# Attention, ELU layer and maxout layer on one core: the engines' orders in the attention stage written out step by step

## The chip, the cores and the metric

The kernel runs on one core of one Trainium2 chip. The metric is the device time of one execution in microseconds (us); lower is better. Three timed runs of the kernel before gave 537.43, 546.26 and 544.27 us, median 544.27 us.

## The reference

```python
# attention: batch 2, 12 heads, 448 tokens, head size 64, fp32
scores = q @ k.T / sqrt(64), causal mask, softmax along the row
x = (attn @ v), heads side by side              # 896 x 768
# first layer: w_in 768 x 2048, w_out 2048 x 768, given in float64
h = x @ w_in
g = where(h > 0, h, exp(min(h, 0)) - 1)         # ELU
x = g @ w_out
# second layer: w1, w2, w3, w_out 768 x 768, given in float64
h = maximum(maximum(x @ w1, x @ w2), x @ w3)
out = h @ w_out                                 # 896 x 768, fp32
```

## The kernel before, in words

**Attention.** The 24 heads are worked in 12 pairs (numbered 0 to 11; 0 to 5 are batch 0). A head has 448 rows, in 4 chunks of 112. A pair goes through these steps, each a small function:

- `load_qk`, `load_v`: transfers of q, k, v on SyncE's queue (SP), the first k on ScalarE's.
- `qk_pe(p, w)`: four TensorE (PE) transposes of q (w=0) or k (w=1) into PSUM (tiles `tq`, `tk`). `qk_copy(p, w)` takes them to SBUF (tile `qk`, three buffers).
- `s_pe(p, g)`: score matmuls of chunk group g, (3), (2, 0) or (1), for both heads (tiles `s`). Four PSUM banks, so two groups at a time.
- `s_max(p, j, c)` on VectorE (DVE, L229): mask, row minimum of the negated scores, result to SBUF tile `e`. `s_exp` on ScalarE (ACT, L243): the exponential with the row's sum. `r_inv` (DVE, L255 and L256): the reciprocals. `e_norm` on GpSimd (POOL, L262): division by the sum.
- `t_pe(p, j, g)`: PE transposes of `e` (tiles `te`, 10 blocks of 112 x 112 a head in groups of 2, 4 and 4). `t_copy` takes them to SBUF (tile `et`).
- `av_pe(p)`: 16 matmul records with v (tile `av`, a single PSUM bank). `x_hi` (ACT, L310) and `x_lo` (DVE, L315) split it into two parts for the next layer (tile `xT`).

The transposes `tq`, `tk` and `te` share three PSUM banks.

**Early part of the first layer.** `d_load`, `d_conv1`, `d_conv2`, `d_hi`, `d_lo` fetch blocks 0 and 1 of w_in and turn float64 into two fp32r parts (tiles `raw_l`, `c_l`, `ws_l`); `d_pe(f, part)` are 12 parts of three matmuls for batch 0 (tile `ph`); `d_elu` and `d_split` are the ELU and the split of its result (tiles `e`, `g`, `gs`).

**What sets the order.** Attention and the early part run under `manual_schedule`: an engine executes its instructions in the order in which the program issues them. In `ORDER` (L414) each kind of step has a number; pair p's step stands at p plus that number, and an engine's line is the sorted list, so that all pairs have the same pattern. `JOIN` (L477) gives the early steps absolute places. `NEEDS` holds a step back in the program until the steps before it are issued. After attention the rest of the first layer, the product with w_out (`py`) and the second layer (`pm`, `po`) are ordered by the tile scheduler. Its first unit is block 0 with batch 1; it uses, as its PSUM bank, the one that `av` had.

Of the kernel before, what the change touches and what calls it, by code (L numbers as in the profile page):

```python
# [9 lines left out]
F32R = mybir.dt.float32r  # L10
# [19 lines left out]
def tile_attention_elu_maxout(  # L30
# [13 lines left out]
    nc = tc.nc  # L44
# [138 lines left out]
    def qk_copy(p, w):  # L183
        if p not in qk_t:
            qk_t[p] = hd.tile([P, 2, S], F32, tag="qk", bufs=3, name=f"qk{p}")
        t = ps_now.pop(("qk", p, w))
        if w == 0:
            nc.scalar.activation(qk_t[p][:, w, :], t[:, :S], AF.Copy, scale=SCALE)  # L188
        else:
            nc.vector.tensor_copy(qk_t[p][:, w, :], t[:, :S])  # L190

    PASSES = ((0, 1),)

# [84 lines left out]
        ps_now["t", h, g] = t[:C, :n], slice(TOFF[grp[0]], TOFF[grp[0]] + n)  # L278


    T_ACT = ((0, 1), (0, 1))
# [38 lines left out]
    def load_win(f, key):  # L320
        raw_t[key] = load64(key, w_in[:, f * P : (f + 1) * P], NW)
# [13 lines left out]
                )  # L335
            yield

    def elu_first(f, b, ph):
# [29 lines left out]

    def d_load(f):
        load_win(f, f"l{f}")  # L370

    def d_conv1(f):
        early["c", f] = conv_first(f"l{f}", raw_t.pop(f"l{f}"), NW)

    def d_conv2(f):
        (low, r), _, high = early.pop(("c", f))
        early["w", f] = conv_last(low, r, high)

    def d_hi(f):
        ws_t[f] = weight_tile(f"l{f}")  # L380
# [12 lines left out]
        if part == KD - 1:  # L393
            drain(early.pop(("gen", f)))

    def d_elu(f):
        early["g", f] = elu_first(f, 0, early.pop(("ps", f)))

    def d_split(f):
        elu_last(f, 0, early.pop(("g", f)), g_early)  # L400

    def drain(gen):
        for _ in gen:
# [2 lines left out]
    def spin(n):  # L406
        for _ in range(n):
# [3 lines left out]

    ORDER = {  # L414
        "SP": {
            (load_qk,): -3.413,
            (load_v,): 0.204,
        },
        "PE": {
            (s_pe, 0): 0.209,  # L420
            (t_pe, 0, 0): 2.025,
            (t_pe, 0, 1): 2.050,
            (s_pe, 1): 0.241,
            (t_pe, 0, 2): 2.323,
            (t_pe, 1, 0): 2.260,
            (s_pe, 2): 0.396,
# [36 lines left out]
            (x_hi,): 3.973,
        },
        "POOL": {
            (e_norm, 0, 3): 1.068,
            (e_norm, 0, 2): 0.924,
            (e_norm, 0, 1): 0.712,
            (e_norm, 0, 0): 1.029,
            (e_norm, 1, 3): 0.153,  # L470
            (e_norm, 1, 2): 0.687,
            (e_norm, 1, 1): 0.924,
            (e_norm, 1, 0): 0.871,
        },
    }

    JOIN = {  # L477
        "SP": {
            (d_load, 0): -0.691,
            (d_load, 1): 3.094,  # L480
            (d_load, 2): 8.233,
        },
        "ACT": {
            (d_conv1, 0): 2.804,
            (d_hi, 0): 3.210,
            (d_conv1, 1): 6.478,
            (d_hi, 1): 9.132,
            (d_elu, 0): 14.736,
            (d_split, 0): 15.039,
            (d_elu, 1): 15.473,  # L490
            (d_split, 1): 15.548,
        },
        "DVE": {
            (d_conv2, 0): 3.345,
            (d_lo, 0): 5.619,
            (d_conv2, 1): 7.954,
            (d_lo, 1): 9.620,
        },
        "PE": {
            (d_pe, 0, 0): 12.269,  # L500
            (d_pe, 0, 1): 12.755,
            (d_pe, 0, 2): 13.105,
            (d_pe, 0, 3): 13.174,
            (d_pe, 0, 4): 13.501,
            (d_pe, 0, 5): 13.589,
            (d_pe, 1, 0): 12.444,
            (d_pe, 1, 1): 14.334,
            (d_pe, 1, 2): 14.066,
            (d_pe, 1, 3): 14.757,
            (d_pe, 1, 4): 14.356,  # L510
            (d_pe, 1, 5): 15.145,
        },
    }


    G_OF = {c: g for g, grp in enumerate(GROUPS_S) for c in grp}
    BOTH = [(j, c) for j in range(2) for c in range(NCH)]
    NEEDS = {
        load_qk: lambda p: [(s_pe, p - 4, 2)],
        load_v: lambda p: [(av_pe, p - 5)],  # L520
        qk_pe: lambda p, w: [(load_qk, p)],
        qk_copy: lambda p, w: [(qk_pe, p, w), (s_pe, p - 3, 2)],
        s_pe: lambda p, g: [(qk_copy, p, 0), (qk_copy, p, 1)]
        + [(s_max, p - (g < 2), j, c) for j in range(2) for c in GROUPS_S[(g + 1) % 3]],
        s_max: lambda p, j, c: [(s_pe, p, G_OF[c]), (t_pe, p - 3, j, 2)],
        s_exp: lambda p, j, c: [(s_max, p, j, c)],
        r_inv: lambda p, j: [(s_exp, p, j, c) for c in range(NCH)],
        e_norm: lambda p, j, c: [(r_inv, p, j)],
        t_pe: lambda p, j, g: [(e_norm, p, j, c) for c in range(min(GROUPS_T[g]), NCH)],
        t_copy: lambda p, j, g: [(t_pe, p, j, g), (av_pe, p - 2)],  # L530
        av_pe: lambda p: [(t_copy, p, j, g) for j in range(2) for g in range(3)]
        + [(x_lo, p - 1)],
        x_hi: lambda p: [(av_pe, p)],
        x_lo: lambda p: [(x_hi, p)],
        d_load: lambda f: [],
        d_conv1: lambda f: [(d_load, f)],
        d_conv2: lambda f: [(d_conv1, f)],
        d_hi: lambda f: [(d_conv2, f)],
        d_lo: lambda f: [(d_hi, f)],
        d_pe: lambda f, part: [(d_lo, f)]  # L540
        + [(s_max, NH // 2 - 1, j, c) for j, c in BOTH],
        d_elu: lambda f: [(d_pe, f, KD - 1)],
        d_split: lambda f: [(d_elu, f)],
    }


    FREES = {
        qk_pe: lambda p, w: (qk_copy, p, w),
        t_pe: lambda p, j, g: (t_copy, p, j, g),
    }  # L550

    def queues():
        for e, steps in ORDER.items():
            line = [(p + at, f, (p, *w)) for (f, *w), at in steps.items() for p in range(NH // 2)]
            line += [(at, f, tuple(w)) for (f, *w), at in JOIN.get(e, {}).items()]
            yield [x[1:] for x in sorted(line, key=lambda x: x[0])]


    with tc.manual_schedule():

        still = const.tile([P, 512], BF16, name="still")
        nc.vector.memset(still, 0.0)
        idle = bank("x", "idle")
        spin(8)

        waiting, issued, frees = list(queues()), set(), [None] * BANKS["t"]
        while any(waiting):
            before = len(issued)
            for line in waiting:
                while line:  # L570
                    f, args = line[0]
                    needs = NEEDS[f](*args) + [frees[turn["t"]]] * (f in FREES)
                    if not all(x in issued for x in needs if x and x[1] >= 0):
                        break
                    if f in FREES:
                        frees[turn["t"]] = FREES[f](*args)
# [179 lines left out]
```

## Time and profile before

| what | value |
|---|---|
| three runs | 537.43, 546.26, 544.27 us; median 544.27 us |
| span of the profiled execution | 537.8 us |
| its own time | the page gives none beside the span; the lowest run is 537.43 us, so what lies around the span is taken as nothing |
| PE busy | 517.2 us (96%) |
| DVE, ACT, POOL busy | 320.2 (60%), 251.7 (47%), 48.5 (9%) us |
| begin of the uninterrupted layer work on PE | 130.27 us |

The last 407.5 us are nearly uninterrupted layer matmuls; the work that the change touches lies in the first 130 us. Shares of busy time over the whole span therefore say little about it. The views by stretch and the chain of waits do.

### The profile page before, as it was taken

How to read it: one execution, taken by the hardware profiler on the slowest of the kernel's cores; microseconds unless marked ns; L12 is line 12 of the kernel's file. 1: busy time of each engine (PE TensorE's matmuls, PEld its weight loads, DVE VectorE, ACT ScalarE, POOL GpSimd, SP SyncE). 2: the span in 40 equal slices, each digit the busy share in tenths (PEclk: the TensorE clock that was granted, in tenths of full speed). 3: DMA queues.
4: the chain of work that ended last, by engine and by line, in shares of the span. 5: the costliest groups of instructions: out<-in, count | busy, mean ns of one | idle time of the engine just before them, and what ended most of it. 6: DMA issues, size and time to landing. Idle time of an engine off the chain costs nothing.

```text
span 537.8 us, 7380 instructions
## 1 busy us (share of the span) xinstructions
PE 517.2 (96%) x2785; PEld 449.1 (84%) x2785; DVE 320.2 (60%) x657; ACT 251.7 (47%) x539; POOL 48.5 (9%) x104
## 2 busy tenths in 40 slices
PE   7869989996999999999999999999999999999997
PEld 3545655675999999999999999999999999999997
DVE  3656888735797778765555555635998857711000
ACT  4657869844576556653332332323544424301111
POOL 1522544520000000000000000000000000000000
PEclk9787999998999999999999999999999999999999
DMA  9932462000456322223333334412566353000111
GB/s 206 218 71 60 96 171 78 18 1 6 121 168 177 99 82 81 84 69 117 100 110 104 118 117 123 152 60 63 205 212 225 118 175 119 1 1 15 62 71 60
DMA packets 75461, 55.53 MB, mean 103 GB/s; under 512 B 34465, under 2 KB 74657, under 8 KB 75425
## 3 DMA queue, kind: packets, MB, share of 16 engines
q1 hardware_dynamic: 74496, 54.83, 34.5%
q8 instruction: 22, 0.36, 0.3%
q10 hardware_dynamic: 928, 0.23, 0.2%
q14 instruction: 15, 0.11, 0.1%
HBM read 52.30 MB, written 2.75 MB: 102 GB/s over the span
## 4 chain that ended last, share of the span: by engine, by line
PE 86%; ACT 9%; DVE 3%; DMA 1%; issue 1%; DVEq 0%; ACTq 0%; SPq 0%
PE pm L333 24%; PE py L636 22%; PE ph L333 22%; PE po L333 8%; ACT e L243 6%; PE s L209 4%; PE te L272 3%; PE av L299 2%; DVE e L229 1%; PE idle L408 1%; DMA raw_l<-in_moe_w_in_dram 1%; ACT et L289 1%; ACT qk L188 1%; DVE c_l L108 0%; PE tk L174 0%
## 5 line engine op out<-in xcount | busy, mean ns | idle before, releaser
L333 PE MATMUL pm<-yT,ws_m 128*128 128x448 f32 x648 | 131.5, 365 | 0.0
L333 PEld LDWEIGHTS pm<-yT,ws_m 128*128 128x128 f32 x648 | 121.7, 188 | 9.6
L333 PE MATMUL ph<-xT,ws_l 128*128 128x448 f32 x576 | 121.4, 372 | 3.8 <-DVE xT L315 3.8
L333 PEld LDWEIGHTS ph<-xT,ws_l 128*128 128x128 f32 x576 | 109.8, 192 | 13.6 <-DVE xT L315 4.2
L636 PE MATMUL py<-gs,ws_o 128*128 128x448 f32 x576 | 116.9, 365 | 0.0
L636 PEld LDWEIGHTS py<-gs,ws_o 128*128 128x128 f32 x576 | 108.2, 188 | 8.5
L243 ACT ACTIVATE e<-e,nm 112x224 f32<-112x224 f32 (+2 forms) x96 | 49.5, 518 | 20.0 <-DVE nm L229 20.0
L262 POOL TENSOR_SCALAR e<-e,r 112x448 f32<-112x448 f32 (+3 forms) x96 | 47.2, 517 | 65.0 <-DVE r L256 40.5
L229 DVE CUSTOM_DVE_ANT_0 e<-s,mask 112x336 f32<-112x336 f32 (+2 forms) x96 | 37.5, 443 | 12.4 <-PE s L209 12.4
L333 PE MATMUL po<-w2s,h 128*128 128x384 f32 x252 | 43.9, 334 | 0.0
L333 PEld LDWEIGHTS po<-w2s,h 128*128 128x128 f32 x252 | 43.7, 188 | 0.0
L272 PE MATMUL te<-ident,e 112*112 112x112 f32 x240 | 33.0, 272 | 5.8 <-ACT qk L188 2.9
L209 PE MATMUL s<-qk 64*112 64x448 f32 (+3 forms) x192 | 34.8, 478 | 3.5 <-ACT qk L188 2.6
L272 PEld LDWEIGHTS te<-ident,e 112*112 112x112 f32 x240 | 24.1, 137 | 14.1 <-issue 6.6
L128 ACT ACTIVATE ws_o<-c_o 128x512 fp32r<-128x512 f32 x24 | 15.1, 629 | 40.5 <-PE py L636 40.5
L209 PEld LDWEIGHTS s<-qk 64*112 64x112 f32 x192 | 18.0, 197 | 17.5 <-issue 8.3
L107 DVE SCALAR_TENSOR_TENSOR c_m<-c_m,raw_m 128x768 uint32<-128x768 uint32 x24 | 22.9, 955 | 15.5 <-ACT c_m L102 15.3
L102 ACT ACTIVATE c_m<-raw_m 128x768 f32<-128x768 f32 x24 | 21.8, 907 | 20.9 <-DVE ws_m L129 15.3
L129 DVE TENSOR_TENSOR ws_o<-c_o,ws_o 128x512 fp32r<-128x512 f32 x24 | 16.5, 689 | 19.3 <-ACT ws_o L128 19.2
L128 ACT ACTIVATE gs<-g 128x448 fp32r<-128x448 f32 x32 | 18.3, 571 | 20.1 <-DVE g L344 20.1
L128 ACT ACTIVATE ws_m<-c_m 128x768 fp32r<-128x768 f32 x18 | 15.2, 845 | 26.2 <-PE pm L333 12.8
L129 DVE TENSOR_TENSOR gs<-g,gs 128x448 fp32r<-128x448 f32 x32 | 19.9, 622 | 11.8 <-ACT gs L128 11.7
(55 smaller groups left out, 488.6 us busy)
## 6 DMA issues: line engine op xcount, KB each, us to landing
raw_m<-in_moe_w_dram SPq DMA_DIRECT2D x18, 768.0 KB, 4.3
raw_l<-in_moe_w_in_dram SPq DMA_DIRECT2D x16, 768.0 KB, 4.7
raw_o<-in_moe_w_out_dram SPq DMA_DIRECT2D x24, 512.0 KB, 3.5
raw_m<-in_moe_w_out_dram SPq DMA_DIRECT2D x6, 768.0 KB, 4.2
qn<-in_q_dram SPq DMA_DIRECT2D x24, 112.0 KB, 3.3
vn<-in_v_dram SPq DMA_DIRECT2D x12, 224.0 KB, 3.3
out_dram<-o SPq DMA_DIRECT2D x14, 192.0 KB, 1.9
kn<-in_k_dram SPq DMA_DIRECT2D x22, 112.0 KB, 3.2
```

The lines of the kernel that those rows point to most:

```text
L102: nc.scalar.activation(f32(r), f32(high), AF.Copy, scale=BIAS),
L107: nc.vector.scalar_tensor_tensor(r, r, 3, low, ALU.logical_shift_left, ALU.bitwise_or)
L128: nc.scalar.activation(hi, src, AF.Copy)
L129: nc.vector.tensor_tensor(lo, src, f32(hi), ALU.subtract)
L209: nc.tensor.matmul(s[j][:C, o : o + (c + 1) * C], qk[:, a, c * C : (c + 1) * C], qk[:, c2, : (c + 1) * C], start=(w == 0 and n == 0), stop ...
L229: nc.vector.tensor_tensor_reduce(out=e_t[h][:, EOFF[c] : EOFF[c] + (c + 1) * C], in0=ps_now.pop(("s", h, c)), in1=mask[:, (NCH - 1 - c) * ...
L243: nc.scalar.activation(e, e, AF.Exp, bias=nm_t[h][:, c : c + 1], scale=-1.0, accum_out=sm_t[p][:, j, c : c + 1],)
L262: nc.gpsimd.tensor_scalar(e, e, ps_now["r", h][:, c : c + 1], 1.0, ALU.mult, ALU.mult)
L272: nc.tensor.transpose(t[:C, n : n + C], e[:, EOFF[c] + j * C : EOFF[c] + (j + 1) * C], ident[:C, :C],)
L299: nc.tensor.matmul(a[j * D : (j + 1) * D, kc * C : S], vn[:, j * NCH + kc, :], et[j][:, TOFF[kc] : TOFF[kc] + S - kc * C], start=(n == 0), ...
L333: nc.tensor.matmul(ps, w(a, kc), x(c, kc), start=(i == 0), stop=(i == len(seq) - 1))
L636: nc.tensor.matmul(py[b][:, :S], w[:, a, kc * P : (kc + 1) * P], g_sp[hk * HK + kc, b][:, c, :], start=(hk == 0 and i == 0), stop=(hk == N ...
```

## The change: what it does

The numbers of `ORDER` and `JOIN` are replaced by `PLAN`, a list for each engine in which each step of each pair stands by itself (a letter for the step, then pair, head or part, and group, in hexadecimal). The pattern can differ from pair to pair. Which engine makes a copy follows from the list in which it stands: 13 of 24 `qk_copy` are on ACT (12 before) and 42 of 72 `t_copy` (48 before). `d_conv1` and `d_conv2` are cut into `d_scale`, `d_shift`, `d_join`; `d_elu` and `d_split` into `d_exp`, `d_max`, `d_ghi`, `d_glo`. The early load of block 2 is left to the scheduler. `NEEDS` and the new `holds` only restate which buffers and banks are in use. What is computed, and the number of matmuls, transposes and copies, stays. On PE the number of places where a step of another kind follows (transposes, scores, `av`, early matmuls) is 66; it was 77. Of these, 25 (before 36) lead into transposes.

```diff
-        if w == 0:
-            nc.scalar.activation(qk_t[p][:, w, :], t[:, :S], AF.Copy, scale=SCALE)
+        o, t = qk_t[p][:, w, :], t[:, :S]
+        if on_act(qk_copy, p, w):
+            nc.scalar.activation(o, t, AF.Copy, scale=SCALE if w == 0 else 1.0)
+        elif w == 0:
+            nc.vector.tensor_scalar(o, t, SCALE, None, ALU.mult)
         else:
-            nc.vector.tensor_copy(qk_t[p][:, w, :], t[:, :S])
+            nc.vector.tensor_copy(o, t)
...
-        if g in T_ACT[j]:
+        if on_act(t_copy, p, j, g):
...
-    ORDER = {
-        "SP": {
-            (load_qk,): -3.413,
-            (load_v,): 0.204,
...
+    PLAN = {
+        "SP": """
+            L0 L1 L2 L3 V0 V1 R0 L4 R1 L5 V2 L6 V3 L7 V4 L8 V5 L9 V6 LA V7 LB V8 V9 VA VB
+            """,
+        "PE": """
+            Q00 Q01 Q11 S02 S00 S01 Q10 Q21 Q20 S12 S11 Q31 Q30 S10 S20 T001 T000 T002 S21 S22
...
+    def on_act(f, *args):
+        return (f, args) in plan["ACT"]
...
+        waiting = [list(line) for line in plan.values()]
```

Three places show what moves. The first is PE after the first pair's scores (`tq1`, `tk1` are q and k of pair 1; `s2`, `s3` the scores of pair 1's heads; `te0` the first transposes of head 0). Before:

```order
L209 MATMUL s0_2_174<-qk0_147 112x224
L209 MATMUL s1_2_175<-qk0_147 112x224
L174 MATMUL tq1_178<-ident_58,qn1_110 128x112 x4
L174 MATMUL tk1_183<-ident_58,kn1_113 128x112 x4
L209 MATMUL s2_0_220<-qk1_195 112x448
L209 MATMUL s3_0_221<-qk1_195 112x448
```

Now:

```order
L174 MATMUL tq1_193<-ident_58,qn1_110 128x112 x4
L174 MATMUL tk2_198<-ident_58,kn2_119 128x112 x4
L174 MATMUL tq2_203<-ident_58,qn2_116 128x112 x4
L212 MATMUL s2_2_236<-qk1_157 112x224
L212 MATMUL s3_2_237<-qk1_157 112x224
L212 MATMUL s2_1_240<-qk1_157 112x336
```

The transposes of pair 2's q and k now stand ahead of pair 1's scores, and pair 3's ahead of the last group of pair 1; k of pair 1 stands ahead of pair 0's scores.

The second is ACT around a copy of q in the middle of attention (`qk6` belongs to pair 6, `e12` and `e13` are its heads; in the second list `qk8` is two pairs later than `e12`). Before:

```order
L243 ACTIVATE e10_646,sm5_648<-e10_646,nm10_647 112x224
L243 ACTIVATE e11_650,sm5_648<-e11_650,nm11_651 112x336
L243 ACTIVATE e11_650,sm5_648<-e11_650,nm11_651 112x224
L243 ACTIVATE e11_650,sm5_648<-e11_650,nm11_651 112x112
L188 ACTIVATE qk6_733<-tq6_710 128x448
L310 ACTIVATE xT0_71<-av2_715 128x448
L289 ACTIVATE et8_770<-te8_0_737 112x224
L289 ACTIVATE et8_770<-te8_1_740 112x448
L243 ACTIVATE e12_762,sm6_764<-e12_762,nm12_763 112x448
```

Now:

```order
L246 ACTIVATE e13_775,sm6_777<-e13_775,nm13_776 112x448
L246 ACTIVATE e12_780,sm6_777<-e12_780,nm12_781 112x336
L189 ACTIVATE qk8_792<-tq8_765 128x448
L290 ACTIVATE et8_836<-te8_1_811 112x448
L246 ACTIVATE e13_775,sm6_777<-e13_775,nm13_776 112x336
L311 ACTIVATE xT0_71<-av3_816 128x448
L246 ACTIVATE e13_775,sm6_777<-e13_775,nm13_776 112x112
```

The copy for a pair's scores stood between the last exponential of the pair before and the first of its own; now it stands two pairs ahead.

The third is DVE at the end of attention (`xT1` is the lower part of x, `av10` and `av11` the last two pairs, `g` and `gs` the early ELU). Before:

```order
L344 SCALAR_TENSOR_TENSOR g_0_0_1537<-e1_0_0_1534,ph0_0_1424 128x448
L315 TENSOR_TENSOR xT1_72<-av10_1511,xT1_72 128x448
L129 TENSOR_TENSOR gs0_0_1553<-g_0_0_1537,gs0_0_1553 128x448
L344 SCALAR_TENSOR_TENSOR g_1_0_1559<-e1_1_0_1556,ph1_0_1438 128x448
L129 TENSOR_TENSOR gs1_0_1561<-g_1_0_1559,gs1_0_1561 128x448
L315 TENSOR_TENSOR xT1_72<-av11_1540,xT1_72 128x448
L103 TENSOR_SCALAR raw_l2_943<-raw_l2_943 128x768
```

Now:

```order
L316 TENSOR_TENSOR xT1_72<-av10_1479,xT1_72 128x448
L316 TENSOR_TENSOR xT1_72<-av11_1530,xT1_72 128x448
L348 SCALAR_TENSOR_TENSOR g_0_0_1553<-e1_0_0_1527,ph0_0_1328 128x448
L348 SCALAR_TENSOR_TENSOR g_1_0_1555<-e1_1_0_1549,ph1_0_1488 128x448
L422 TENSOR_TENSOR gs0_0_1557<-g_0_0_1553,gs0_0_1557 128x448
L422 TENSOR_TENSOR gs1_0_1559<-g_1_0_1555,gs1_0_1559 128x448
L103 TENSOR_SCALAR raw_l2_1573<-raw_l2_1573 128x768
```

Both x parts stand ahead of the ELU. The conversion of block 2 (`raw_l2`) still stands behind all of it.

## Rows read from the trace of the kernel before

**Rows 1.** The page's head line.

```profile
span 537.8 us, 7380 instructions
```

**Rows 2.** Busy time by stretch: length, engines (instructions), granted clock, DMA share, GB/s.

```profile
13.10:19.90 6.80, 6.05 (x26) 3.95 (x26) 3.97 (x21) 4.21 (x16) 3.83 (x8) 0.50 1.06 211
...
40.40:47.20 6.80, 6.00 (x25) 3.47 (x25) 3.83 (x12) 4.05 (x14) 3.16 (x7) 0.50 0.30 67
47.20:129.10 81.90, 76.37 (x577) 49.91 (x575) 55.40 (x203) 59.76 (x191) 32.53 (x66) 1.00 0.24 64
129.10:136.00 6.90, 5.73 (x15) 5.12 (x16) 4.46 (x6) 1.55 (x2) 0.00 (x0) 0.51 0.27 73
```

**Rows 3.** Chain of waits, 7 to 47 us: start us, us, what.

```profile
7.42 0.99 PE s L209 x4
...
9.17 4.20 ACT e L243 x16
13.38 0.43 ACT qk L188
...
13.85 1.89 PE s L209 x4
...
43.52 3.26 PE s L209 x12
```

**Rows 4.** Chain of waits, 69 to 86 us, one pair's TensorE work, and a transfer.

```profile
69.19 1.70 PE s L209 x12
70.89 1.10 PE te L272 x10
71.99 0.57 PE s L209 x4
72.56 0.53 PE te L272 x4
73.09 0.38 PE tq L174 x4
73.47 2.04 PE av L299 x16
75.51 0.55 PE tk L174 x4
...
79.84 4.66 DMA raw_l<-in_moe_w_in_dram
```

**Rows 5.** Chain of waits, 108 us to the layer work.

```profile
108.88 0.62 PE ph L333 x3
...
114.10 0.72 PE te L272 x6
...
116.06 0.96 PE te L272 x10
...
122.96 0.54 DVE xT L315
...
123.55 2.13 PE av L299 x16
...
129.68 0.54 DVE xT L315
...
130.27 69.74 PE ph L333 x330
```

**Rows 6.** Waits, 0 to 131 us: who, for whom: us, times, longest.

```profile
ACT e L243 <- DVE nm L229: 20.0, 12, 3.1
```

**Rows 7.** Stretch of 101 to 111 us, tile `te` alone: PE, PEld, DVE, ACT, clock, DMA.

```profile
101.00:111.00 10.00, 4.83 (x38) 3.64 (x39) 1.84 (x3) 3.31 (x8) 1.00 0.01 2
```

**Rows 8.** Conversion of block 2 in order of time, from 130 us.

```profile
130.13 0.56 DVE L103 TENSOR_SCALAR raw_l<-raw_l 128x768 uint32<-128x768 uint32 x1
...
132.78 0.84 ACT L128 ACTIVATE ws_l<-c_l 128x768 fp32r<-128x768 f32 x1 [2.97 <-DVE c_l L108]
...
133.65 0.96 DVE L129 TENSOR_TENSOR ws_l<-c_l,ws_l 128x768 fp32r<-128x768 f32 x1 [0.91 <-ACT ws_l L128]
```

More of the change, by code (lines that the diff above doesn't have):

```diff
@@ L370, in d_load, with d_scale, d_shift, d_join @@
         load_win(f, f"l{f}")
[L372 to L377, printed above, removed]
+        early["raw", f] = raw_t[f"l{f}"]
+    def d_scale(f):
+        raw = raw_t.pop(f"l{f}")
+        c = cv.tile([P, NW], U32, tag="c", bufs=2, name=f"c_l{f}")
+        early["c", f] = raw[:, :, 0], c, raw[:, :, 1]
+        nc.scalar.activation(f32(c[:, :]), f32(raw[:, :, 1]), AF.Copy, scale=BIAS)
+    def d_shift(f):
+        low = early["raw", f][:, :, 0]
+        nc.vector.tensor_scalar(low, low, 29, None, ALU.logical_shift_right)
+    def d_join(f):
+        early["w", f] = conv_last(*early.pop(("c", f)))
     def d_hi(f):
@@ L394, in d_pe, with d_exp, d_max, d_ghi @@
             drain(early.pop(("gen", f)))
[L396 to L400, printed above, removed]
+    def d_exp(f):
+        early["e", f] = elu_exp(f, 0, early["ps", f])
+    def d_max(f):
+        early["g", f] = elu_max(f, 0, early.pop(("e", f)), early.pop(("ps", f)))
+    def d_ghi(f):
+        g_sp[f, 0] = g_early.tile([P, 2, S], F32R, tag=f"g{f}_0", name=f"gs{f}_0")
+        nc.scalar.activation(g_sp[f, 0][:, 0], early["g", f], AF.Copy)
+    def d_glo(f):
+        gs = g_sp[f, 0]
+        nc.vector.tensor_tensor(gs[:, 1], early.pop(("g", f)), f32(gs[:, 0]), ALU.subtract)
     def drain(gen):
@@ L513, in tile_attention_elu_maxout @@
+    STEP = {
+        "L": load_qk, "V": load_v, "R": d_load, "Q": qk_pe, "S": s_pe, "T": t_pe, "A": av_pe,
+        "D": d_pe, "M": s_max, "I": r_inv, "C": t_copy, "K": qk_copy, "Y": x_lo, "X": x_hi,
+        "E": s_exp, "N": e_norm, "a": d_scale, "b": d_shift, "c": d_join, "h": d_hi, "l": d_lo,
+        "e": d_exp, "f": d_max, "g": d_ghi, "k": d_glo,
     }
     G_OF = {c: g for g, grp in enumerate(GROUPS_S) for c in grp}
-    BOTH = [(j, c) for j in range(2) for c in range(NCH)]
+    T_OF = [(j, g) for j in range(2) for g in range(3)]
@@ L518, in tile_attention_elu_maxout @@
     NEEDS = {
-        load_qk: lambda p: [(s_pe, p - 4, 2)],
+        load_qk: lambda p: [(qk_pe, p - 4, w) for w in range(2)],
         load_v: lambda p: [(av_pe, p - 5)],
         qk_pe: lambda p, w: [(load_qk, p)],
[L522 to L525, printed above, removed]
+        qk_copy: lambda p, w: [(qk_pe, p, w)] + [(s_pe, p - 3, g) for g in range(3)],
@@ L526, in tile_attention_elu_maxout @@
+        s_pe: lambda p, g: [(qk_copy, p, w) for w in range(2)],
+        s_max: lambda p, j, c: [(s_pe, p, G_OF[c])] + [(t_pe, p - 3, j, g) for g in range(3)],
         s_exp: lambda p, j, c: [(s_max, p, j, c)],
@@ L530, in tile_attention_elu_maxout @@
         t_copy: lambda p, j, g: [(t_pe, p, j, g), (av_pe, p - 2)],
-        av_pe: lambda p: [(t_copy, p, j, g) for j in range(2) for g in range(3)]
-        + [(x_lo, p - 1)],
+        av_pe: lambda p: [(load_v, p), (x_lo, p - 1)] + [(t_copy, p, *t) for t in T_OF],
         x_hi: lambda p: [(av_pe, p)],
@@ L535, in tile_attention_elu_maxout, with holds, issued_all @@
         d_load: lambda f: [],
-        d_conv1: lambda f: [(d_load, f)],
-        d_conv2: lambda f: [(d_conv1, f)],
-        d_hi: lambda f: [(d_conv2, f)],
+        d_scale: lambda f: [(d_load, f)],
+        d_shift: lambda f: [(d_load, f)],
+        d_join: lambda f: [(d_scale, f), (d_shift, f)],
+        d_hi: lambda f: [(d_join, f)],
         d_lo: lambda f: [(d_hi, f)],
[L540 to L543, printed above, removed]
-    }
-    FREES = {
-        qk_pe: lambda p, w: (qk_copy, p, w),
-        t_pe: lambda p, j, g: (t_copy, p, j, g),
-    }
[L552 to L556, printed above, removed]
+        d_pe: lambda f, part: [(d_lo, f), (x_lo, part), (d_pe, f, part - 1)],
+        d_exp: lambda f: [(d_pe, f, KD - 1)],
+        d_max: lambda f: [(d_exp, f)],
+        d_ghi: lambda f: [(d_max, f)],
+        d_glo: lambda f: [(d_ghi, f)],
+    }
+    def holds(f, args):
+        if f is qk_pe:
+            return [("t", [(qk_copy, *args)])]
+        if f is t_pe:
+            return [("t", [(t_copy, *args)])]
+        if f is s_pe:
+            p, g = args
+            return [("s", [(s_max, p, j, c) for c in GROUPS_S[g]]) for j in range(2)]
+        if f is d_pe and args[1] == 0:
+            return [("s", [(d_max, args[0])])]
+        return []
+    plan = {
+        e: [(STEP[w[0]], tuple(int(d, 16) for d in w[1:])) for w in line.split()]
+        for e, line in PLAN.items()
+    }
+    def on_act(f, *args):
+        return (f, args) in plan["ACT"]
+    def issued_all(needs):
+        return all(x in issued for x in needs if min(x[1:]) >= 0)
     with tc.manual_schedule():
@@ L564, in tile_attention_elu_maxout @@
         spin(8)
-        waiting, issued, frees = list(queues()), set(), [None] * BANKS["t"]
+        issued, busy = set(), {}
+        waiting = [list(line) for line in plan.values()]
         while any(waiting):
@@ L571, in tile_attention_elu_maxout @@
                     f, args = line[0]
-                    needs = NEEDS[f](*args) + [frees[turn["t"]]] * (f in FREES)
-                    if not all(x in issued for x in needs if x and x[1] >= 0):
+                    held = [
+                        ((kind, (turn[kind] + n) % BANKS[kind]), by)
+                        for n, (kind, by) in enumerate(holds(f, args))
+                    ]
+                    needs = NEEDS[f](*args) + [x for b, _ in held for x in busy.get(b, [])]
+                    if not issued_all(needs):
                         break
-                    if f in FREES:
-                        frees[turn["t"]] = FREES[f](*args)
+                    busy.update(held)
                     f(*args)
```

142 lines of the change are left out of this document (47 added, 95 removed).

## The prediction

> **What bounds the kernel now.** The first look goes to the span, 537.8 us [rows 1], and to the point from which TensorE (PE) only runs layer matmuls, 130.27 us [rows 5]. From there to the end are 407.5 us that the change leaves alone but for their first blocks. So the question is when that point comes; I call it T.
>
> The second look is the chain of waits ahead of T. At the start it goes round a loop: scores of pair 0 at 7.42 us, eight exponentials with their sums on ScalarE (ACT) in 4.20 us, the copy of pair 1's q at 13.38, only then pair 1's scores at 13.85 [rows 3]. The copy stands behind all exponentials of the pair before, and ACT has nothing to do until the new scores come: it waited 20.0 us for row minima, in 12 waits, one a pair [rows 6]. In the middle the loop is still there, but PE is nearly full as well. At the end the chain leaves PE twice for the x parts of VectorE (DVE): `av` of pair 11 starts at 123.55 behind one that ended at 123.50, and the layer work at 130.27 behind one that ended at 130.22 [rows 5].
>
> The third look is the stretches. From 47.2 to 129.1 us PE is busy 76.4 of 81.9 us, ACT 59.8, DVE 55.4, at full clock (2.4 GHz). In three other stretches the granted clock is 0.50 or 0.51, the 1.2 GHz level [rows 2].
>
> **PE's own work, as a floor for T.** One pair without a gap: scores 1.70 and 0.57, transposes of e 1.10, 0.53 and 0.72 (10, 4 and 6 of them), of q and k 0.38 and 0.55, `av` 2.04 [rows 4, 5]. That is 7.59 us, and 91.1 for 12 pairs. The early matmuls are 12 parts of 0.62, 7.4 us [rows 5]. The first scores start at 7.42, with pair 0's q and k (0.93) already done. 7.42 + 91.1 - 0.9 + 7.4 = 105.0 us. Before, T was 130.27: 25.3 us of the way were waits and half clock.
>
> **The change, part by part.**
>
> *Fewer changes of kind.* Ten transposes took 1.10 us behind scores and 0.96 behind early matmuls [rows 4, 5]; the first of a run behind another kind costs 0.14. 11 fewer places lead into transposes: 1.5 us less. The places that lead elsewhere are 41 in both, so I count nothing for them. Floor: 103.5 us.
>
> *The copies of q and k ahead.* The loop is cut. Walking the new lists by hand with the rows' durations: up to the first transposes of e, PE has 7.42 + 6 x 0.38 + two pairs of scores (4.5) + one group (0.99), that is until 15.2 us; the exponentials of head 0 are then about ready, as ACT runs through them from 9.2 with two copies between. So PE finds work nearly all the time. I did the same for the stretch from pair 6's scores to pair 8's: seven transpose steps follow each other over three banks, and each finds its bank free with about 0.3 us to spare. For what such a walk misses at the start I take 2.0 us, with ends of 0 and 6.4 (twice the 3.2 us that PE stood between the scores of pairs 0 and 1: 6.43 less 2.27 and 0.93). ACT and DVE have room: if the same 59.8 and 55.4 us fell into the shorter time that PE needs, 76.4, they would be busy 78% and 73%.
>
> *Clock.* Twelve score records take 3.26 us at half clock [rows 3] and 1.70 at full [rows 4]. Each of the two stretches of 6.8 us held 6.0 us of PE work [rows 2], so each cost up to 3.0. I take one of them as staying, 3.0, with ends of 0 and 6.0.
>
> *The conversion of block 4 on DVE.* The scheduler puts its first step (L103) into DVE's list some dozen rows behind the step that frees its buffer, and its transfer took 4.66 us in the chain [rows 4]. By my walk DVE has 3.5 us of work in between. Stall 1.1 us, ends 0 and 4.7; the copies behind it on DVE hold transpose banks, so it counts for PE.
>
> *The end.* `av` of pair 11 is followed by three early parts, 1.86 us, while ACT and DVE make the two x parts in about 1.2 us: the layer work follows without a gap. The 4.2 us that PE stood there are part of the 25.3 above.
>
> T = 103.5 + 2.0 + 3.0 + 1.1 = 109.6 us.
>
> *Behind T.* The first 5.7 us of layer work ran at half clock [rows 2, 5], which cost 2.85; with no gap ahead of T this goes. But it covered something. The conversion of blocks 2 and 3 still stands behind the early ELU. At full clock PE needs block 2 after 36 matmuls of 0.203 (69.74 less 2.85, over 330 [rows 5]), at T + 7.3. DVE and ACT need about 3.0 for block 1's ELU (from 126.7 to 129.7 in the chain), then 0.56, two steps of the length of the last, 0.84 for the upper part and 0.96 for the lower [rows 8]: 7.3, just in time. Block 3, with block 4's steps mixed in between, comes out at T + 16.1 while PE wants its lower part at T + 15.0. I put 1.2 us back, ends 0 and 3.
>
> Sum: 109.6 + 407.5 - 2.85 + 1.2 = 515.5 us, 22.3 less than the profiled execution. This one stood with the lowest of the three runs (537.43), 6.5 below their median of 544.27. If the others lost their time where the change does not reach, the median becomes 522; if they lost it in the loop, nearer 515.5. I take the middle, **519 us**.
>
> **A rule that speaks against it.** Transposes of e held PE for 4.83 of 10 us from 101 to 111, and the clock stayed at 1.00 [rows 7]. Half clock I see where PE had just stood: from 13.1 us, as it waited for the scores at 13.85 [rows 2, 3], and behind the gap ahead of T [rows 2, 5]. The Trainium skill, "TensorE: Matmul & The Clock Gate", Part 4 (PE-mode transpose), says that transposes do not count as busy in the same way and that the full clock does not engage for them. By that rule the new runs of up to seven transpose steps would pull the clock down; this trace does not agree with it for runs mixed with scores, `av` and early matmuls. It is the third rival below.
>
> **The rivals.**
>
> 1. *Order good, engines not that exact: 522 to 529 us, chance 0.12.* PE waits for copies in the transpose runs, since each of three banks needs its copy from an engine that has other steps first. If half of the 25.3 us stays, T is 103.5 + 12.7 = 116.2, and the end 522 by the profile, 528.5 by the median. For it: before, too, PE had 5.5 us without work between 47.2 and 129.1 [rows 2]. Against: the hand walks.
>
> 2. *Only the end gains: 532 to 538 us, chance 0.14.* The start is held by the transfers (DMA share above 1 from 13.1 to 19.9 [rows 2]), with both weight blocks now issued ahead of pair 5's q and k, and the middle by PE, which is nearly full already. Then 4.2 + 2.85 - 1.2 = 5.9 us go: 531.9 by the profile, 538.4 by the median. Against: no transfer of q or k is in the chain; the new list fetches pair 3 ahead of the weights.
>
> 3. *Slower: the half clock stays through attention, chance 0.06.* Place: PE between 7.4 us and T. At half clock 1.70 us of scores took 3.26, so a us of work costs 0.9 more. To be 2% slower than the median (555.2, against 522) needs 33 us, that is 37 us of PE's work, some 70 us of half clock. The three stretches shown have 20.5 [rows 2]. If all 96 us of work were at half clock, T would be near 190 and the end near 600. Below 70 us of half clock this ends within 2%.
>
> That the change does less than it says I exclude but for rival 2: the lists are executed as they stand.
>
> **How the numbers follow.** Forecast 0.68, rivals 0.12, 0.14, 0.06. The low end is the floor with nothing put back: 103.5 + 404.65 = 508 us. With all upper ends T is 103.5 + 6.4 + 6.0 + 4.7 = 120.6 and the end 528 by the profile, 535 by the median. Range 508 to 535; left out are the upper half of rival 2, rival 3 and a little below the floor. Two per cent (10.9 us) is about what a measurement of this kernel can tell from no change, its three runs lying 8.8 us apart. Below 533.4: forecast and rival 1, 0.80. Within 2%: rival 2 and a third of rival 3, 0.16. Slower: 0.04.
>
> **What would show it.** In the changed kernel's trace: the first scores of pair 4 well before 43.5 us (by PE's work about 26); ACT's wait for row minima far below 20 us; PE over 95% busy from 20 us to T; no gap of PE between the last `av` and the layer work; T between 104 and 120; at most one stretch of half clock behind 10 us; a wait of PE for `ws_l` of about 1 us some 14 us behind T. The prediction is wrong if PE shows many waits for `et` or `qk` copies, if the chain goes through transfers of q or k, or if the clock is at half where PE is full.

## The result, and the profile after

Four runs of the changed kernel took 518.87, 511.96, 518.82 and 519.03 us, median **518.85 us**; four of the kernel before 537.43, 546.26, 544.27 and 546.49 us, median 545.26 us. The ratio is **0.956** (95% interval 0.946 to 0.966). The runs of both kernels lie on two levels, 7 to 9 us apart (the last section says where 7 of them are): lower against lower, one run each, the change is worth 25.5 us (537.43 to 511.96), upper against upper, medians of three, 27.4 us (546.26 to 518.87).

Below, T is again the point from which TensorE runs only layer matmuls, 130.27 us before [rows 5].

The page of the kernel after: head line, TensorE (busy us, share, instructions), and its granted clock in 40 slices.

```profile
span 517.1 us, 7412 instructions
...
PE 510.3 (99%) x2785; PEld 441.3 (85%) x2785; DVE 318.8 (62%) x662; ACT 251.5 (49%) x534; POOL 50.4 (10%) x104
...
PEclk9999999999999999999999999999999999999999
```

The chain of waits of the kernel after at the end of attention, the answer to [rows 5].

```profile
94.60 2.04 PE av L300 x16
96.64 0.81 PE ph L334 x3
97.44 1.34 PE te L275 x14
...
100.23 2.04 PE av L300 x16
102.27 2.04 PE ph L334 x9
```

Behind the last row (the early parts that are left) TensorE goes on with batch 1 without a gap: T is 102.27 + 2.04 = 104.3, 26.0 us earlier than before. (Matmuls overlap, and batch 1's first one starts at 104.1, the value that some expectations below name.) The waits of the kernel after from 0 to 131 us, the answer to [rows 6]:

```profile
ACT e L246 <- DVE nm L232: 1.1, 2, 0.9
...
PE te L275 <- POOL e L265: 0.7, 2, 0.4
...
PE ph L334 <- DVE ws_l L129: 0.7, 1, 0.7
...
PE tk L174 <- DMA kn<-in_k_dram: 0.5, 1, 0.5
```

ScalarE's 20.0 us are down to 1.1, and behind its first 2 us no wait of TensorE is above 0.7 us. The stretches of the kernel after, with the columns of [rows 2]:

```profile
20.00:30.00 10.00, 10.00 (x87) 6.95 (x84) 9.51 (x40) 9.88 (x35) 7.98 (x16) 1.00 1.09 209
30.00:40.00 10.00, 10.00 (x81) 6.13 (x81) 9.85 (x35) 9.97 (x35) 5.80 (x12) 1.00 1.02 194
...
50.00:60.00 10.00, 9.59 (x79) 6.42 (x76) 8.37 (x30) 9.94 (x32) 5.71 (x9) 1.00 0.18 34
...
110.00:120.00 10.00, 9.67 (x46) 8.11 (x44) 7.78 (x11) 6.78 (x12) 0.00 (x0) 1.00 0.34 90
```

From 20 to 40 us three engines are nearly full at once, and the clock is 1.00 throughout. Before, it was at half in the two stretches of [rows 2] that lie ahead of T, in a third from 30.2 to 33.6 us (0.50, not among those rows), and around T.

### The profile page after: what moved, and what is told of

Read it like the earlier page. It is cut to its first block, busy times and chain, and to the rows that moved or that the text cites. A ratio compares the mean times of both kernels' runs of the same rounds, so it can differ in the third digit from the quotient of the medians.

```text
span 517.1 us, 7412 instructions
## 1 busy us (share of the span) xinstructions
PE 510.3 (99%) x2785; PEld 441.3 (85%) x2785; DVE 318.8 (62%) x662; ACT 251.5 (49%) x534; POOL 50.4 (10%) x104
## 4 chain that ended last, share of the span: by engine, by line
PE 92%; DVE 3%; DMA 2%; POOL 1%; issue 1%; SPq 0%; ACT 0%; DVEq 0%; ACTq 0%; POOLq 0%
PE pm L334 26%; PE py L628 23%; PE ph L334 20%; PE po L334 8%; PE te L275 4%; PE av L300 4%; PE s L212 4%; DVE e L232 1%; POOL e L265 1%; DMA raw_l<-in_moe_w_in_dram 1%; PE tk L174 1%; DMA kn<-in_k_dram 1%; PE tq L174 1%; DVE c_l L107 1%; SPq L155 0%
## 5 line engine op out<-in xcount | busy, mean ns | idle before, releaser
L334 PE MATMUL pm<-yT,ws_m 128*128 128x448 f32 x648 | 134.1, 368 | 0.0
L628 PE MATMUL py<-gs,ws_o 128*128 128x448 f32 x576 | 119.2, 368 | 0.0
L334 PEld LDWEIGHTS ph<-xT,ws_l 128*128 128x128 f32 x576 | 107.1, 188 | 13.8 <-DVE ws_l L129 1.3
L265 POOL TENSOR_SCALAR e<-e,r 112x224 f32<-112x224 f32 (+3 forms) x96 | 49.1, 532 | 45.7 <-DVE r L259 20.6
L246 ACT ACTIVATE e<-e,nm 112x112 f32<-112x112 f32 (+3 forms) x96 | 49.5, 520 | 1.2 <-DVE nm L232 1.1
L232 DVE CUSTOM_DVE_ANT_0 e<-s,mask 112x224 f32<-112x224 f32 (+3 forms) x96 | 38.3, 441 | 4.5 <-PE s L212 3.7
L102 ACT ACTIVATE c_m<-raw_m 128x768 f32<-128x768 f32 x24 | 21.9, 911 | 18.7 <-DVE ws_m L129 13.0
L275 PE MATMUL te<-ident,e 112*112 112x112 f32 x240 | 30.0, 264 | 0.7 <-POOL e L265 0.7
L212 PE MATMUL s<-qk 64*112 64x224 f32 (+3 forms) x192 | 28.8, 417 | 0.3 <-DVE nm L232 0.2
L691 DVE TENSOR_TENSOR mx<-pm,mx 128x448 f32<-128x448 f32 x24 | 14.9, 621 | 21.0 <-PE pm L334 21.0
L102 ACT ACTIVATE c_o<-raw_o 128x512 f32<-128x512 f32 x24 | 16.0, 665 | 21.6 <-DVE ws_o L129 19.2
```

Of the source, the lines that this page charges most:

```text
L102: nc.scalar.activation(f32(r), f32(high), AF.Copy, scale=BIAS),
L212: nc.tensor.matmul(s[j][:C, o : o + (c + 1) * C], qk[:, a, c * C : (c + 1) * C], qk[:, c2, : (c + 1) * C], start=(w == 0 and n == 0), stop ...
L232: nc.vector.tensor_tensor_reduce(out=e_t[h][:, EOFF[c] : EOFF[c] + (c + 1) * C], in0=ps_now.pop(("s", h, c)), in1=mask[:, (NCH - 1 - c) * ...
L246: nc.scalar.activation(e, e, AF.Exp, bias=nm_t[h][:, c : c + 1], scale=-1.0, accum_out=sm_t[p][:, j, c : c + 1],)
L265: nc.gpsimd.tensor_scalar(e, e, ps_now["r", h][:, c : c + 1], 1.0, ALU.mult, ALU.mult)
L275: nc.tensor.transpose(t[:C, n : n + C], e[:, EOFF[c] + j * C : EOFF[c] + (j + 1) * C], ident[:C, :C],)
```

## Where the 26 us came from, and what all kernels showed

Cut T in three by the scores' records on TensorE (192 in all, 16 for a pair): *start*, to the 65th, with which pair 4 begins; *middle*, to the 177th; *end*, from there to T. All numbers are us from one profiled execution each; the last column is the span behind T.

```
kernel                        65th  middle  end   T      span - T
before                        43.5  58.5    28.3  130.3  407.5
after                         24.8  52.9    26.6  104.3  412.8
e1  before, x first           42.3  58.2    24.6  125.1  407.3
e2  after, x last             24.8  52.9    34.0  111.7  404.9
e3  before, copies ahead      42.0  57.0    28.5  127.5  413.3
e4  after, weights swapped    25.4  52.8    26.6  104.8  405.8
e5  e3 + scores ahead of te   36.8  57.8    29.5  124.1  407.6
e6  start before, then after  43.7  50.1    26.6  120.4  405.7
e7  start after, then before  35.8  59.2    28.3  123.3  406.5
e8  e5 + e1 + ACT's ws_l      32.6  58.1    25.9  116.6  407.3
e12 e8 + DVE's c_l placed     33.9  55.1    25.8  114.8  407.2
e13 after, ACT's ws_l early   24.9  57.8    26.6  109.3  405.7
```

The change gained 18.7 us in the start, 5.6 in the middle and 1.7 at the end. Two cautions go with the table. The parts do not hold the same work: up to the 65th score record TensorE runs 46 records of `te` and 16 of `tk` in `before`, but 22 and 12 in `after`, so some 2.8 us of the 18.7 (0.096 for a `te`, 0.55 for four `tk`) are work that `after` does later. And one order does not give the same times in every execution: e1, whose edit touches only the end, has a start 1.2 us shorter than `before`, while e9 and e10, which have the order of `after` up to T, reach it at 104.5 and 104.6 us (104.3). A difference of about 1 us in the start says nothing.

The experiments ask which waits these were.

## The experiments

**e1, e2: x at the end, done alone and undone.** In `before` the ELU of block 0 is held until the last x is written; in `after` the x parts go back behind the ELU.

```diff
# e1, on before
-            (d_elu, 0): 14.736,
+            (d_elu, 0): 14.980,
-        d_elu: lambda f: [(d_pe, f, KD - 1)],
+        d_elu: lambda f: [(d_pe, f, KD - 1), (x_lo, NH // 2 - 1)],
# e2, on after: DVE, then ACT
-            CB10 CB11 YA YB f0 f1 k0 k1
+            CB10 CB11 f0 YA k0 f1 k1 YB
-            e0 XB e1 g0 g1
+            e0 XB g0 e1 g1
```

> The kernel before with one thing of the change: both x parts of pairs 10 and 11 stand ahead of the early ELU on ACT and DVE. T is the point from which PE only runs layer matmuls (130.3 us in the profile of before, 104.1 in that of the change). Theory (the end was worth about 4 us of gap and a stretch of half clock): the last av follows the early parts at once, T = 126.5, no half clock behind it, 5 to 7 us less than before (ratio about 0.988). Rival A (the end is the larger part of the gain): T below 122. Rival B (the gap at the end only moves): T within 1 us of 130.3.

> The changed kernel with one thing undone: on ACT and DVE the early ELU stands ahead of the x parts of pairs 10 and 11 again, as before. Theory: PE stands for an ELU chain (two exponential steps, maximum, split, split, x part) behind the early parts, T = 108, with possibly a stretch of half clock behind the gap; the blocks' conversion behind T is then better covered. 3 to 7 us more than the change (ratio 1.006 to 1.014). Rival A: more than 8 us. Rival B: within 1 us.

e1: median 534.3 us (four runs, 533.21 to 535.91), ratio to before 0.989 (0.983 to 0.994). TensorE at the end of attention in e1, in order of time:

```profile
121.73 2.11 PE L299 MATMUL av<-et,vn 112*64 112x448 f32 x16
123.76 0.88 PE L333 MATMUL ph<-xT,ws_l 128*128 128x448 f32 x3
125.14 2.09 PE L333 MATMUL ph<-xT,ws_l 128*128 128x448 f32 x9 [0.49 <-DVE xT L315]
```

Of the last gap 0.49 us are left, and the granted clock behind it is 1.00. T is 5.2 us earlier, 3.7 of them in the end. e2: four runs of 518.38, 518.56, 527.45 and 527.72 us, the lowest 6.4 above the lowest of `after`; T is 7.4 us later (111.7, where 108 was expected). TensorE's waits and two stretches of e2:

```profile
PE ph L334 <- DVE xT L316: 3.7, 1, 3.7
PE av L300 <- DVE xT L316: 2.1, 1, 2.1
```

```profile
103.00:106.40 3.40, 3.40 (x17) 2.01 (x14) 0.00 (x0) 0.87 (x2) 0.00 (x0) 0.50 0.00 0
...
111.70:115.00 3.30, 3.30 (x16) 3.08 (x17) 2.30 (x3) 0.82 (x1) 0.00 (x0) 1.00 0.00 0
```

The two waits are 5.8 us, and the clock falls to half behind the earlier one (2.1 us, up to 102.2). Behind the later and longer one (3.7 us, up to 111.7) it stays at 1.00. So this one part is worth 4 to 7 us by itself. The end column shows less, 1.7, since `after` has more left to do behind its 177th score record: 60 records of `te` and 80 of `av` against 54 and 64 before, some 2.6 us by their rows (0.096 each, 2.04 for 16).

**e4: the order of loads.** The weight blocks and pairs 3 to 6 back in the queue's order of before, with the block that `after` converts first still loaded first.

```diff
-            L0 L1 L2 L3 V0 V1 R0 L4 R1 L5 V2 L6 V3 L7 V4 L8 V5 L9 V6 LA V7 LB V8 V9 VA VB
+            L0 L1 L2 R1 L3 V0 L4 V1 L5 V2 L6 R0 V3 L7 V4 L8 V5 L9 V6 LA V7 LB V8 V9 VA VB
```

> The changed kernel with SyncE's queue as before at the start: the first weight block ahead of pair 3's q and k, the second behind pair 6's (the block that this kernel converts first is loaded first). Theory (transfers were not what held the start): T within 1.5 us of 104.1. Rival (the order of the loads is a part of the gain): PE waits for pair 3's k or q, or DVE and ACT for a block, and T is 3 us later or more.

One run, 512.38 us, T 104.8, 0.5 us later and within the theory's 1.5. The order of loads is no visible part of the gain.

**e3: copies of q and k one pair earlier in `before`.**

```diff
-            (qk_pe, 0): -0.256,
-            (qk_pe, 1): -0.095,
+            (qk_pe, 0): -1.256,
+            (qk_pe, 1): -1.095,
# and (qk_copy, 1) -0.195 to -1.195, (qk_copy, 0) -0.077 to -1.077
```

> The kernel before with four numbers of the order changed: the transposes of q and k and their copies stand one pair earlier (one less in each number); nothing else. Theory (the loop exponentials, copy of q, scores, row minimum, exponentials is what held the start and the middle): ACT's wait for row minima falls from 20 us to below 6, and T from 130.3 to between 112 and 120; a ratio of 0.965 to 0.98. Rival (the gain needs the step by step order; the loop is only where the waits show): T stays above 125, with the waits put down to something else, as transposes' banks or copies.

My theory fell: median 536.96 us (ten runs), ratio 0.994 (0.990 to 0.999), T only 2.8 us earlier, and ScalarE still waits 16.3 us for row minima. The chain of e3 says why:

```profile
39.01 1.86 ACT e L243 x8
40.87 0.44 ACT qk L188
41.30 0.04 issue
41.35 0.71 PE te L272 x4
42.06 3.22 PE s L209 x12
```

Moved by a whole pair, the copy of q stands where it stood: on ScalarE behind a pair's last exponentials. It is another pair's q now, but the copy frees the PSUM bank that the next `te` waits for, and the scores stand behind that `te` on TensorE. A wait for data had become a wait for a bank; e5 tests that. It is not the only one in this chain: just ahead of it ScalarE waited 3.0 us for the weight block's `c_l`, a wait that comes back below.

**e5: the same, with the scores ahead of the `te` in TensorE's list.**

```diff
-            (s_pe, 0): 0.209,
+            (s_pe, 0): 0.005,
-            (s_pe, 1): 0.241,
+            (s_pe, 1): 0.010,
```

> The kernel before with its copies of q and k one pair earlier (as in e3), and in TensorE's list the scores of a pair's first group placed ahead of the te transposes, whose bank the q copy frees. Theory (the 20 us in which ACT waited for row minima came from scores that stand behind a late q copy, in e3 still by way of the bank): ACT's wait for nm falls below 10 us, the layer work begins at T between 112 and 120 (127.47 in e3, 130.27 before), the time is T + 406, 518 to 526 us at the short spacing of matmuls, 7 us more at the long one. Rival (a pattern that is the same for all pairs can not do better than before, since start and middle want different orders): T stays above 124 and the wait above 14 us.

One run, 533.54 us. ScalarE's waits in e5:

```profile
ACT e L243 <- DVE nm L229: 4.7, 5, 1.7
ACT ws_l L381 <- DVE c_l L108: 2.8, 1, 2.8
```

The wait for minima went from 16.3 to 4.7 us as the theory said, but T, 124.1, missed its 112 to 120 (and just meets the rival's "above 124"): 11.6 us of waits bought 3.4 of T. The start did gain 5.2 us on e3, but the middle and the end came out 0.8 and 1.0 us longer, and TensorE still waits 3.8 us for x at the end, as in e3. What limits the start now is the next wait, in the chain of e5:

```profile
31.16 1.15 DVE c_l L107
...
32.33 1.01 DVE c_l L108
...
33.36 0.84 ACT ws_l L381
34.20 1.16 ACT e L243 x4
...
36.87 1.70 PE s L209 x12
```

ScalarE stands for block 0's `c_l` with exponentials behind it, and pair 4's scores come last.

**e6, e7: the two orders spliced at pair 4's scores.** e6 has the lists of `before` up to V4 (SP), T201 (PE), C201 (ACT), I31 (DVE), N203 (POOL), then what is left in the order of `after`; e7 the lists of `after` up to V4, S30, C110, K41, N200, then the order of `before`.

```diff
# e6, PE behind the cut, against before
- A0 Q41 T200 T201 S40 S41 T210 T202 T211 S42 T212 Q50 A1
+ A0 Q41 T200 T201 S41 Q51 S42 T210 T212 T202 Q50 A1 S40
# e7, PE behind the cut, against after
- T110 Q40 A0 S30 S41 T100 T111 T112 Q51 T101 S42 T210 T102
+ T110 Q40 A0 S30 T100 T101 T102 T111 T112 T200 T201 S40 S41
# e7, ACT behind the cut, against after
- E300 E202 X0 C110 a1 C100 C111 C112 E311 E310 E313 C102
+ E300 E202 X0 C110 a0 C100 C101 E303 h0 E313 E302 C111
```

> The order of before up to the first scores of pair 4, from there the changed order with its end. Theory (most of the gain, 18.7 of 26.2 us, was made ahead of pair 4's scores; the rest in the middle and at the end): pair 4's first scores come at 42 to 44 us, T lies between 118 and 125, the time T + 406, 524 to 531 us at the short spacing. Rival (the changed order behind pair 4 makes up for a late start, since the engines then have the same work left and catch up): T below 115.

> The changed order up to the first scores of pair 4, from there the order of before with its own end. Theory (the start is worth about 18.7 us by itself): pair 4's first scores come near 25 us, T lies between 109 and 116, the time T + 406, 515 to 522 us at the short spacing. Rival (the order of before cannot use the head start, since its engines wait for each other at the same places and its transfers come at the same times): T above 120.

e6: one run, 527.88 us, T 120.4 as expected: with the old start 16.1 of the 26 us are lost, and the order behind it does not make up for them. e7: one run, 531.61 us, T 123.3; my theory (109 to 116) fell, and the rival's T above 120 came. Up to pair 3 (49th record) e7 is as early as `after` (19.6 against 19.4 us), then pair 4 comes at 35.8. ScalarE's wait in e7 from 18 to 40 us, and the stretch of 28 to 38:

```profile
ACT ws_l L395 <- DVE c_l L108: 4.0, 1, 4.0
```

```profile
28.00:38.00 10.00, 6.01 (x26) 4.24 (x28) 4.96 (x11) 5.33 (x18) 1.73 (x5) 0.50 1.02 252
```

The same step as in e5, ScalarE's `ws_l` of block 0 in the order of before, stands in the chain again. It is not all: TensorE had waited 1.6 us for GpSimd, in two waits just ahead of it, the clock is at half from 28 us on, and the step from pair 3 to pair 4 takes 16.2 us, longer than in either kernel (13.4 and 5.4), so part of it may come from the seam of the two orders. How much each cost is not shown, and what the start is worth by itself stays open in e7. The weight step gave the next two kernels.

**e13: this wait put into `after`; e8: taken out of `before`.** In `after` ScalarE's step h1 stands at 59 us, 26 us behind the `c_l` that it reads. e13 moves this one entry to 29 us. e8 is e5 with the x order of e1, and ScalarE's step on block 0 a pair later.

```diff
# e13, on after, ACT
-            a1 C100 C111 C112 E311 E310 E313 C102 C212 E312 E302 E301
+            a1 C100 C111 C112 E311 E310 E313 C102 C212 h1 E312 E302 E301
...
-            X4 E712 E713 C510 E710 h1 E711 K91 E811
+            X4 E712 E713 C510 E710 E711 K91 E811
# e8, on e5 and e1
-            (d_hi, 0): 3.210,
+            (d_hi, 0): 4.210,
```

> The changed kernel with one entry of ACT's list moved: its step on block 1 (h1, ws_l from c_l) stands right behind the copy at 29 us instead of at 59 us, so that ACT waits there for DVE's c_l, which is made at 30.7 to 32.7 us. Theory (such a wait of 3 us with exponentials and copies queued behind it was part of what the kernel before lost in its start, and it is lost on an ACT that is busy 9.97 of 10 us): ACT waits 2.5 to 3 us for c_l, the scores of pair 5 and later come 1.5 to 3 us later, T at 106 to 107.5 (104.3). Rival (PE sets the pace there and ACT's lists have slack for it): T below 105.

> The kernel before with one pattern for all pairs still, and three of its waits taken away: copies and scores as in e5, both x parts of the last pair ahead of the early ELU as in e1, and ACT's step on block 0 (ws_l), which waited 2.8 us for DVE's c_l in e5 with exponentials and copies behind it, one pair later. Theory (gains of start and end are separate waits and add up): pair 4's first scores at 33 to 35 us (36.8 in e5), from pair 11's scores to T 24 to 26 us (29.5 in e5), T between 114 and 118, no wait of ACT for c_l. Rival (in the start each engine is only a little behind another, and the next wait takes the place of ACT's): pair 4 at 36 us or later, T between 118.5 and 121, by the end alone.

e13: one run, 516.79 us. Waits of ScalarE (from 20 to 100 us) and of TensorE (up to 116 us), and a stretch of e13:

```profile
ACT ws_l L395 <- DVE c_l L108: 2.6, 1, 2.6
...
PE s L212 <- ACT qk L189: 3.0, 1, 3.0
```

```profile
37.00:40.40 3.40, 3.40 (x22) 2.48 (x22) 2.51 (x12) 3.02 (x11) 1.81 (x4) 0.66 1.05 299
```

T is 5.0 us later, 1.8 more than the theory's upper end: it priced the wait (2.6 us, 3.0 on TensorE) but not the slower clock behind it (0.66 from 37.0 to 40.4). e8: one run, 525.69 us; no wait for `c_l` is left in the start, the 65th record comes at 32.6 (36.8 in e5), the end is 25.9 (29.5), T 116.6. The end and T are as expected, the start 0.4 us better. (The expectation of e12 below names 115.4 as T of e8; by the table's measure it is 116.6.) In its middle one step of a pair took 11.0 us; the chain of e8 there:

```profile
66.80 0.86 DVE c_l L107
...
68.88 0.61 DVE e L229
...
69.56 1.25 PE s L209 x4
```

**e12: e8 with VectorE's `c_l` where VectorE waits for exponentials.**

```diff
-            (d_conv2, 0): 3.345,
+            (d_conv2, 0): 3.667,
-            (d_conv2, 1): 7.954,
+            (d_conv2, 1): 7.667,
```

> The kernel of the three repairs (e8) with DVE's two-instruction step c_l (1.9 us) of both early blocks placed ahead of the reciprocals, where DVE waits for ACT's exponentials, instead of right ahead of a pair's first row minima. Theory (in e8 that step held minima and then scores at 29 to 32 and at 67 to 69 us): pair 4 at 30.5 to 32 us (32.6), the step from pair 8's to pair 9's scores 8.5 to 9.5 us (11.0), T at 111 to 114 (115.4). Rival (the wait goes to the copy of k and to x, which stand behind it now): T at 115 or later.

One run, 523.77 us. Right for block 1 (pairs 8 to 9 in 8.2 us instead of 11.0, middle 55.1), wrong for block 0: the start did not gain (33.9 against 32.6, hardly more than two executions differ by). T 114.8 lies just outside either expectation.

With one pattern for all pairs, then, four small moves bring T from 130.3 to 114.8. Of the 10.5 us to `after`, 9.1 lie in the start, some 2.3 of them again work that `after` does later (22 records of `te` and 12 of `tk` there, 40 and 16 in e12). In the start `after` has transposes of the next two pairs ahead of a pair's scores. That this prefetch is what they need I argue from the lists; no kernel here had it alone.

**e9: transposes alone.** Behind attention in `after`, 240 transposes by themselves.

```diff
+        run = bank("t", "run")
+        for _ in range(240):
+            nc.tensor.transpose(run[:C, :C], e_t[2 * (NH // 2 - 1)][:, :C], ident[:C, :C])
```

> The changed kernel with 240 more transposes of 112 x 112 (e against the identity, into one bank, read by nobody) alone on TensorE right behind attention; everything else is as it was. Theory (transposes keep the clock up like other work here): about 0.1 us each, 24 us in all, at a granted clock of 1.00 in that stretch and behind it; the layer work begins near 128. Rival (the Trainium skill, TensorE: Matmul & The Clock Gate, Part 4: the full clock does not engage for transposes): the granted clock falls to 0.5 in the stretch, the transposes take twice as long, some 45 us, and the first layer matmuls behind them show 0.5 as well.

The chain of e9, then a stretch of nothing but transposes and the one behind:

```profile
104.50 23.00 PE run L575 x240
127.50 2.65 PE ph L334 x13
```

```profile
115.30:127.30 12.00, 12.00 (x129) 12.00 (x127) 0.20 (x1) 0.00 (x0) 0.00 (x0) 1.00 0.01 1
127.50:137.50 10.00, 10.00 (x51) 9.25 (x51) 4.37 (x7) 4.31 (x7) 0.00 (x0) 1.00 0.00 0
```

0.096 us each at a granted clock of 1.00, in 23 us of nothing else, and 1.00 behind. The rule of the Trainium skill that the forecast weighed ("TensorE: Matmul & The Clock Gate", Part 4), that the full clock does not engage for transposes, does not hold for these fp32 transposes: they kept it. Whether transposes alone would raise the clock from half, no run shows.

**e10: the price of a change of kind.** Behind attention 48 transposes, 48 score matmuls (two records each), then 12 times 4 of one and 4 of the other.

```diff
+        turn_round(48)
+        score(48)
+        for _ in range(12):
+            turn_round(4)
+            score(4)
+        turn_round(8)
```

> The changed kernel, and behind attention on TensorE alone: 48 transposes of 112 x 112, 48 matmuls like one head's scores (112 x 448), then 12 times 4 of one and 4 of the other, and 8 transposes; nothing reads their results. Theory of the forecast (a place that leads into transposes costs 0.14 us): the stretch of 12 alternations takes 1.6 to 2.0 us more than the two plain stretches together. Rival (a change of kind costs nothing by itself, and the 0.14 us in attention were waits of a sequencer for something else): under 0.5 us more.

The chain of e10 (`run` L579 transposes, L583 scores):

```profile
104.61 4.60 PE run L579 x48
109.21 36.26 PE run L583 x96
145.47 0.53 PE run L579 x4
145.99 3.19 PE run L583 x8
...
190.03 0.91 PE run L579 x8
```

Four transposes take 0.53 us instead of 4 x 4.60 / 48 = 0.38, eight score records 3.19 instead of 8 x 36.26 / 96 = 3.02. A change costs 0.15 us into transposes and 0.17 into scores. The 12 rounds ended at 190.03, so they took 44.6 us, 3.7 more than the plain 40.9 and twice what the theory said; I had counted one direction only.

## Why the prediction was right, step by step

- **The mechanism** was as forecast: with better orders TensorE's own work is the bound up to T. The floor was 103.5, T came out at 104.3. Pair 4's first scores came at 24.8 us (forecast 26); ScalarE's wait for minima fell from 20.0 to 1.1; TensorE is full from 20 us on but for 50 to 70 us (9.6 and 9.7 of 10).
- **The three allowances on the floor** (2.0 for the start, 3.0 for half clock, 1.1 for VectorE) were mis-sized, 6.1 us against 0.8. The start lost 0.5 us to a transfer of k; no stretch of half clock came at all, and TensorE's longest wait between the first scores and T was 0.4 us; 0.7 us went to waits for GpSimd, which I had not named; of VectorE's conversion ahead of T nothing shows. These waits make 1.2 us, more than the 0.8, so TensorE's work itself came out a little below the floor; the next point says why it may have.
- **Changes of kind**: the 1.5 us were mis-sized too, most likely too small. The 0.14 us were read off ten transposes behind scores (1.10) against ten behind early matmuls (0.96), but these are another kind as well, and 0.96 is just 10 x 0.096: behind early matmuls a run of transposes cost nothing extra. Behind scores it is 0.15 (e10). Into other kinds I had counted nothing, as their number stayed at 41 (77 - 36 before, 66 - 25 now), but e10 puts 0.17 on a place that leads from transposes into scores, and by the lists there were 22 of these and are 12. From scores into transposes it is 22 and 17. At e10's prices that makes an estimate of 10 x 0.17 + 5 x 0.15 = 2.5 us, without the places behind `av` (10 and 1), which e10 did not price.
- **Behind T**: the give-back for the weight conversion (1.2 us forecast) came where it was forecast, some 15 us behind T, with 0.7 us. TensorE in the kernel after:

```profile
118.65 1.03 PE L334 MATMUL ph<-xT,ws_l 128*128 128x448 f32 x3
120.39 0.88 PE L334 MATMUL ph<-xT,ws_l 128*128 128x448 f32 x3 [0.71 <-DVE ws_l L129]
```

- **405.9 us behind T was wrong for this execution** (412.8): its layer matmuls came at the wider spacing of the last section. On the narrower one it would be near 405.8, as in e4, which has the same work there. So the forecast's 522 by the median and 515.5 by the profile turned out as the two levels, measured as 518.9 and 511.96: both 3 to 3.5 us lower than forecast, T being 5.3 lower and the time around the span (518.87 - 517.1 = 1.8), taken as nothing, higher. The 519 was the middle between them, where no run of either level is expected. That it hit the median of 518.85 is luck: both values were 3 us too high, and three of the four runs lay on the upper level.
- **Rivals.** Waits for copies (1) did not come: none of TensorE for `et` or `qk` shows up to T. "Only the end gains" (2) is refuted by the start's 18.7 us, and its held transfers by e4; half clock (3) by the profile of after, and for transposes by e9.

## What to carry to other kernels

Look for what is queued behind a waiting instruction on a busy engine: one weight step of 0.84 us, moved 30 us forward in ScalarE's list to a place where its input came 2.6 us later, cost 5.0 us of 104 (e13). When a copy is moved earlier, follow its bank as well as its data (e3), and expect the next wait behind the one removed: 11.6 us less of waiting gave 3.4 us (e5). A wait of TensorE can cost twice, by itself and by the slower clock behind it (2.1 us in e2, 3.0 in e13), but need not (3.7 us in e2).

## What was not expected of the hardware

The same layer matmuls run at one of two spacings, fixed for an execution, at a granted clock of 1.00 in both. The product with w_out (`py`, 576 matmuls with no idle time before them) in the kernel before, and in the kernel after:

```profile
L636 PE MATMUL py<-gs,ws_o 128*128 128x448 f32 x576 | 116.9, 365 | 0.0
```

```profile
L628 PE MATMUL py<-gs,ws_o 128*128 128x448 f32 x576 | 119.2, 368 | 0.0
```

The difference is 2.3 us for 576, 4.0 ns each; over the 1,764 matmuls of `ph`, `py` and `pm` behind T that is 7 us. The 252 of `po` start 173 ns apart in both. The stretch of 300 to 330 us in the kernel before, in the kernel after, and in e4, which has the steps of after but for its loads:

```profile
300.00:330.00 30.00, 30.00 (x150) 27.81 (x149) 16.35 (x28) 9.19 (x15) 0.00 (x0) 1.00 0.33 105
```

```profile
300.00:330.00 30.00, 30.00 (x147) 27.25 (x146) 15.20 (x23) 8.77 (x13) 0.00 (x0) 1.00 0.46 149
```

```profile
300.00:330.00 30.00, 30.00 (x150) 27.81 (x149) 16.14 (x23) 8.77 (x14) 0.00 (x0) 1.00 0.43 138
```

TensorE is full in all three, with 150, 147 and 150 matmuls. In the table's last column after and e3 are on the wide spacing (413 us), all others on the narrow one (405 to 408), so it goes with the execution and not with the kernel. What sets it stays open. A comparison of single profiles across spacings is off by 7 us; T is not.
